# Layer out by seven block products of 288 columns in place of eight, and a new order for the first two batches

## The chip, the cores and the metric

The kernel runs on one core of one Trainium2 chip. The time is device microseconds of one launch. The engines are TensorE (PE; its weight loads are PEld), VectorE (DVE), ScalarE (ACT), GpSimd (POOL) and SyncE (SP), which issues the DMAs. Each engine works through its own instructions in order.

## What is computed

An attention over 32 packed queries, an attention of the long queries over the packed result, and an expert layer with a maximum of three products:

```python
p_packed = sm_attn(p, k, v)                  # 8 batches, 8 heads, 576 keys, 32 packed, 64 wide
out = sm_attn(q, p_packed, p_packed)         # 576 queries per head
x = out.transpose(0, 2, 1, 3).reshape(8 * 576, 512)
h = np.maximum(np.maximum(x @ w1, x @ w2), x @ w3)   # 768 hidden
return h @ w_out                                      # 768 -> 512
```

`sm_attn` is softmax attention with scale 1/8. All is float32. The last line, `h @ w_out`, is what the text calls Layer out; the three products before it are Layer in.

## The kernel before

The eight batches go through the same stages one after another, with the stages of the next batch laid between the matmuls of this one. Results are kept transposed: columns are the 576 tokens of a batch, rows the features.

- **Attention.** `scores` (S) multiplies packed queries and keys, `weigh` (A) takes the softmax, `spread` (X) or `turn` transposes it, `values` (V) and `packed` (K) give the packed result, `queries` (Q) multiplies it with the long queries, and `attend` (B) takes their softmax e and turns it, then splits it into a high part (a2h, a copy in the type float32r) and a low part (a2l, the difference). A product of two float32 operands is made of three float32r matmuls: high by high, low by high, high by low.
- **Weights.** `load_w` brings 24 pieces of 512 words by DMA, `convert` (C) turns each into float32 (two ACT instructions, one DVE, one POOL). The pieces of w_out are also split there into `wo_hi` and `wo_lo`.
- **Layer in.** `project` (P) folds the packed result of a batch into the input weights of one hidden slice j (128 of the 768 rows, so j = 0..5); result pw, split into ph and pl. `layer_in` (N) then computes, for each half of 288 columns and each of the three weights, six matmuls of 288 columns into one PSUM bank (tile mi). `maximum` (E) copies the first of three banks out and takes the maximum with the other two (tile hf).
- **Layer out.** `halves` (H) splits the first 512 of the 576 columns of a slice into high and low part; the last 64 columns go into `tails`, where the 64 of all eight batches stand side by side as 512 columns. `layer_out` (O) adds up each of four output blocks of 128 rows over six slices: 4 x 6 x 3 = 72 matmuls of 512 columns a batch (tile mo). They are issued in twelve "thirds" of 6 (`THIRDS`). After the last batch the same 72 matmuls run once more on the tails, as a ninth set. `finish` (F) scales a block out of PSUM and stores it.

PSUM has two double banks (`ps_big`) for attention and projections, and four single banks (`ps_moe`) for mi, mo and some projections.

**Order.** The first two batches are ordered by hand: `START` is a list of words that sets the order on every engine. A word names a stage with its numbers (`N03`: Layer in of batch 0, slice 3) and issues its next step; a trailing v, g or a moves that step's elementwise instruction to DVE, POOL or ACT; `I10` puts ten matmuls of no use ahead of the next step, to keep TensorE running; k, v, q and w words are loads. For batches 2 to 7 only TensorE's order is fixed: `STAGES` gives the tick, counted from the start of a batch, at which each stage of the next batch is due (`S1:7`: scores of the next batch at tick 7; P6 to P8 are slices 0 to 2 of the next batch). A batch has 36 ticks of Layer in, one for each group of six matmuls, and then one for each step of Layer out. `halves` of a slice is begun one tick after its Layer in. The other engines are ordered by the compiler's scheduler, by the order of issue. Each tile comes from a pool with a tag; the tiles of one tag share a fixed number of buffers, and a new tile waits until one is free.

## Time and profile before

| | us |
|---|---|
| median of 3 runs | 482.0 |
| lowest and highest | 481.85, 482.4 |
| span of the profiled execution | 480.7 |
| outside the span (482.0 - 480.7) | 1.3 |
| busy PE, DVE, ACT, POOL | 471.3, 254.1, 192.5, 130.6 |

The span runs from the first to the last instruction of one execution. The profiled execution has no time of its own beside its span, so the median of the runs stands for it. Rows of the profile give a line of the code, the engine, the operation and "out<-in" by tile names; busy times are in us, means in ns. "idle before" tells how long the engine waited and for which engine. A piece of the chain of waits reads: start, length, engine, tile, line, number of instructions.

### The profile page before, as it was taken

What the parts mean: (1) busy time and instruction counts of PE and PEld (TensorE: products, weight loads), DVE (VectorE), ACT (ScalarE), POOL (GpSimd) and SP (SyncE); (2) the same over time, 40 slices, a digit from 0 to 9 for tenths busy, and PEclk for the clock granted to TensorE, in tenths of its full rate; (3) what the DMA queues carried; (4) which work ended last, traced back from release to release, by engine and by line L of the source; (5) the groups of instructions that cost most, each with busy time, mean ns of one, the idle gap of its engine ahead of it and who ended that gap; (6) DMA issues with size and microseconds to landing.
All of it is one profiled execution on the core that took longest, in us unless ns stands there. A gap on an engine that the chain in (4) does not pass through costs nothing.

```text
span 480.7 us, 10562 instructions
## 1 busy us (share of the span) xinstructions
PE 471.3 (98%) x4352; PEld 388.8 (81%) x4352; DVE 254.1 (53%) x546; ACT 192.5 (40%) x415; POOL 130.6 (27%) x108
## 2 busy tenths in 40 slices
PE   8889999999999999999999999999999999999997
PEld 3367999888778887899789887899778887899885
DVE  2899988833646465453726455363826456244100
ACT  3687854401344334432434325342434324343211
POOL 0666754600322222122212213122222214244000
PEclk9999999999999999999999999999999999999999
DMA  8999221664244152233313142243310201100122
GB/s 302 399 376 407 95 87 65 219 176 147 74 164 128 34 176 81 82 98 110 122 66 125 36 145 100 73 120 107 124 68 12 40 2 45 44 1 1 44 67 65
DMA packets 36767, 55.60 MB, mean 116 GB/s; under 512 B 21488, under 2 KB 23792, under 8 KB 36720
## 3 DMA queue, kind: packets, MB, share of 16 engines
q1 hardware_dynamic: 36720, 54.93, 34.3%
q8 instruction: 34, 0.56, 0.5%
q14 instruction: 13, 0.11, 0.1%
HBM read 41.94 MB, written 9.44 MB: 107 GB/s over the span
## 4 chain that ended last, share of the span: by engine, by line
PE 93%; DMA 5%; ACT 0%; SPq 0%; issue 0%; DVE 0%; ACTq 0%
PE mi L450 48%; PE mo L504 32%; PE pw L414 7%; DMA wi<-in_wi 2%; PE av L312 2%; PE s L341 2%; DMA q<-in_qt 1%; DMA v<-in_va 1%; PE s L226 1%; PE tp L312 0%; PE tp L269 0%; SPq L160 0%; ACT wi L189 0%; PE av L327 0%; ACT a L244 0%
## 5 line engine op out<-in xcount | busy, mean ns | idle before, releaser
L450 PE MATMUL mi<-a2h,ph 128*128 128x288 f32 x576 | 174.1, 302 | 0.0
L450 PE MATMUL mi<-a2h,pl 128*128 128x288 f32 x576 | 169.8, 295 | 0.3 <-DVE pl L427 0.3
L450 PE MATMUL mi<-a2l,ph 128*128 128x288 f32 x576 | 169.7, 295 | 0.0
L465 DVE TENSOR_TENSOR hf<-mi,hf 128x288 f32<-128x288 f32 x192 | 86.6, 452 | 108.1 <-PE mi L450 90.3
L504 PE MATMUL mo<-h,wo_hi 128*128 128x512 f32 x432 | 140.3, 398 | 0.0
L450 PEld LDWEIGHTS mi<-a2h,ph 128*128 128x128 f32 x576 | 108.0, 188 | 14.6 <-issue 9.2
L450 PEld LDWEIGHTS mi<-a2h,pl 128*128 128x128 f32 x576 | 108.1, 188 | 1.0 <-DVE pl L427 0.7
L450 PEld LDWEIGHTS mi<-a2l,ph 128*128 128x128 f32 x576 | 108.1, 188 | 0.0
L131 POOL TENSOR_TENSOR h<-hf,h 128x512 fp32r<-128x512 f32 x36 | 46.6, 1295 | 214.8 <-ACT h L126 119.9
L504 PEld LDWEIGHTS mo<-h,wo_hi 128*128 128x128 f32 x432 | 81.0, 187 | 26.1 <-issue 4.2
L504 PE MATMUL mo<-h,wo_lo 128*128 128x512 f32 x216 | 85.3, 395 | 0.0
L427 DVE SCALAR_TENSOR_TENSOR pl<-pw,ph 128x768 fp32r<-128x768 f32 (+1 forms) x60 | 45.9, 788 | 26.8 <-ACT ph L425 26.6
L126 ACT COPY hf<-mi 128x288 f32<-128x288 f32 x83 | 33.0, 398 | 62.7 <-PE mi L450 57.7
L126 ACT CAST h<-hf 128x512 fp32r<-128x512 f32 x45 | 27.8, 620 | 69.4 <-DVE hf L465 69.4
L524 ACT ACTIVATE o<-mo 128x512 f32<-128x512 f32 x32 | 19.1, 597 | 75.7 <-PE mo L504 58.2
L425 ACT ACTIVATE ph<-pw 128x768 fp32r<-128x768 f32 (+1 forms) x60 | 38.3, 680 | 25.4 <-PE pw L414 25.3
L504 PEld LDWEIGHTS mo<-h,wo_lo 128*128 128x128 f32 x216 | 40.5, 188 | 8.9
L414 PE MATMUL pw<-w_sb,pt 64*32 64x384 f32 x768 | 38.1, 488 | 0.7 <-ACT a L244 0.7
L204 POOL TENSOR_TENSOR w_sb<-w_sb,wi 128x512 int32<-128x512 int32 x18 | 24.1, 1348 | 26.7 <-DVE w_sb L200 18.7
L370 POOL TENSOR_TENSOR e<-e,m 128x576 f32<-128x576 f32 (+1 forms) x15 | 16.7, 1129 | 34.2 <-DVE m L368 34.2
L131 POOL TENSOR_TENSOR a2l<-et,a2h 128x576 fp32r<-128x576 f32 (+1 forms) x13 | 17.5, 1346 | 21.0 <-ACT a2h L126 20.9
L414 PEld LDWEIGHTS pw<-w_sb,pt 64*32 64x32 f32 x768 | 12.0, 106 | 13.3 <-issue 10.6
(91 smaller groups left out, 338.6 us busy)
## 6 DMA issues: line engine op xcount, KB each, us to landing
kt<-in_kp SPq DMA_DIRECT2D x16, 640.0 KB, 5.0
wi<-in_wi SPq DMA_DIRECT2D x18, 512.0 KB, 7.8
out_t<-o SPq DMA_DIRECT2D x35, 256.0 KB, 2.0
v<-in_va SPq DMA_DIRECT2D x16, 512.0 KB, 4.6
q<-in_qt SPq DMA_DIRECT2D x14, 576.0 KB, 5.8
wo<-in_wo SPq DMA_DIRECT2D x6, 512.0 KB, 6.9
xt<-x SPq DMA_DIRECT2D x48, 40.0 KB, 2.0
xt<-x SPq DMA_DIRECT2D x48, 32.0 KB, 1.9
```

Of the source, the lines that this page charges most:

```text
L126: e.copy(out=out, in_=src)
L131: on(default).tensor_tensor(out=lo, in0=src, in1=hi.bitcast(F32), op=ALU.subtract)
L204: nc.gpsimd.tensor_tensor(out=dst.bitcast(I32), in0=dst.bitcast(I32), in1=up, op=ALU.add)
L312: nc.tensor.matmul(out=ps[r][NP * i:NP * i + NP, :], lhsT=at[r][0:n, t, i], rhs=loaded["v", b, g][0:n, t, h * D:(h + 1) * D], start=(t == ...
L370: on("g").tensor_tensor(out=e3, in0=e3, in1=m.unsqueeze(2).to_broadcast([P, nt, NP]), op=ALU.subtract)
L414: nc.tensor.matmul(out=ps[r][NP * n:NP * n + NP, 0:NW * P], lhsT=pt_sb[b % 2][o, NP * n:NP * n + NP], rhs=w_sb[o, j, n * NW * P:(n + 1) * ...
L425: nc.scalar.activation(out=hi[:, r], in_=x, func=AF.Copy, scale=2.0 ** -WS)
L427: nc.vector.scalar_tensor_tensor(out=lo[:, r], in0=x, scalar=2.0 ** -WS, in1=hi[:, r].bitcast(F32), op0=ALU.mult, op1=ALU.subtract,)
L450: nc.tensor.matmul(out=sums[b, j, hf, x][:, 0:HS], lhsT=w[:, r, x * P:(x + 1) * P], rhs=a[:, c], start=(r == 0 and n == 0), stop=(r == R - ...
L465: nc.vector.tensor_tensor(out=h, in0=sums[b, j, hf, i][:, 0:HS], in1=h, op=ALU.max)
L504: nc.tensor.matmul(out=sums[b, m], lhsT=w[:, j, m * P:(m + 1) * P], rhs=h[:, a], start=(j == 0 and i == 0), stop=(j == NJ - 1 and i == 2),)
L524: nc.scalar.activation(out=o, in_=ps, func=AF.Copy, scale=2.0 ** -WS)
```

## The change

Layer out multiplies a matrix of 512 x 768 with one of 768 x 576 per batch. Each pair of slices, both output halves (256 rows) and both column halves (288) make a 2 x 2 block product. In place of its 8 block products, 7 products of sums and differences of blocks are computed (a Strassen scheme with 15 additions), each added up over the three slice pairs.

- `weights` (W) makes the seven combinations of each pair's weight blocks once, with their high and low parts.
- `maximum` writes the four blocks of a slice pair into one tile r. `halves` makes, after the even slice, one difference and the high and low part ya (2 blocks); after the odd slice yb (2 blocks), two instructions of differences, and yc (3 blocks).
- `layer_out` issues fourteen steps, seven products by two halves of 128 rows, of 9 matmuls with 288 columns, in the order 1, 5, 2, 6, 7, 4, 3. Products 1 and 5 read ya, 2 and 3 yb, 6, 7 and 4 yc.
- `finish` scales products 1 and 5 out of PSUM on ACT, adds the others to earlier results on DVE, and makes two more sums on POOL.
- All 576 columns of a batch are covered, so `tails` and the ninth set are gone.
- The pool has new tags: `b` (8 buffers) for k, v, q, the turned softmax and r; `y` (21) for attention, ya, yb and the results; `xs` (6) for loaded weights and later for the weight combinations; `yt` (6) for yc.
- `START` and `STAGES` are new. In the new `START` the fourteen steps of batch 0 lie between and behind the last Layer in steps of batch 1, and the fourteen of batch 1 at its end.

The removed bodies of `halves`, `layer_out` and `finish`, printed above, are left out of the diff; so are changes of a tag alone.

```diff
-SM = SF * P
 SR = S - SF * P
+NQ = NJ // 2
+MH = DM // 2
 NT = S // NP
 NW = 3
 WC = 512
-NST = 4
 WS = 8
+NX, NB, NY = 6, 8, 21
...
-k01 k00 w00 I10 S0 A01 v00 v01 w02 C00 A01 A00 A00 I7 A01 A01v A00 q000 q010 C00 w01 I1 V01 C00 C00 A00v
-Z00 Z01 q011 C02 V01 V00 q001 V00 w21 K0 K0v C02 C01 I1 Q0 C02 B000 B000 B010 C01 C02 B010 B000g C01
-B000 B010v w11 w10 B000 w12 I8 Q0 B000a B010 C21 B001 B000 C21 C01 I3 P00 B011 B000g B001 B001g P00 B011
-B000 C21 B011v B000a B000g C21 B001 B011 B010 B001 B010a B011 B010 k10 k11 C10 B001a w20 P00 I10 N00
-B011a B001 B011 B001v B010v w32 w22 C10 C11 C10 I4 S1 B011v B010 B001 C12 C11 B010a C10 B011 B010v C11
-C12 P00 C12 P00 B001a C20 N00 A10 N00 B011a v11 v10 C20 C11 A11 C12 A10 w40 A11 P01 B001v q10 q11 E000v
-B011g E000 Z11 P01 C32 C32 C20 Z10 C20 A10 N00 N00 P01 C32 A10v A11 N00 C22 A11a E001v C40 C22 E000 V101
-E001 V101 C32 N01 w30 w31 K1 C22 w61 E001 C22 C40 K1a H00a N01 w62 Q1 C30 E010v C40 H00v B11 B10 C40 C30
-H00v N01 C30 C30 C31 N01 E010 B10 P02 P02 E010 C31 P10 B10g E011v w42 P02 N01 w63 C31 N01 B11 C61 w41
-C31 E011 w60 B10 C42 E011 N02 C42 N02 P03 H01a N02 C42 N02 B10 E020v C42 B10v E020 H01g P03 C41 E021a
-N02 N02 B11g E020 P03 C41 E021 H01v C41 N03 N03 C41 P10 B10 P10 E021 H02v E030v C61 B11 B11 E030 N03 w52
-w51 w50 P11 P04 B10g C61 B11v C52 C62 E030 N03 C62 P04 C50 H02g N03 P04 B11 C63 H02a E031a B10 E031 N03
-B10a N04 N04 E040a B11g C51 N04 E031 B11 E040 B10v C51 C51 B11a N04 B11v C50 C52 E041a N04 N04 H03a C61
-E040 E041 E041 N10 H03v C62 C50 C52 H03a E100v H04a P11 N10 N10 C50 E100 C51 P11 E100 N10 C63 E101a N10
-N10 N11 E101 H04v H04a E110v N11 N11 E110 C52 P05 P12 E101 N11 N11 P05 C61a H10a P05 E111a C60 P12 C62
-E110 N11 C61g H10v E111 N05 E111 H11v P12 C60 C62a H10a E050a N05 N05 E050 N05 N12 E051v H11g E050 C62v
-N05 N05 P13 P14 E051 N12 H11v E051 C60 E120a P14 H05v C63 N12 w64 w65 P13 H05g E120 C63 C60 N12 N12 N12
-P13 E121a C65 E120 H05v N13 C63v E121 E121 E130a H12a q21 k20 k21 C64 C60a C65 P14 C64 N13 N13 C63g H12g
-C60g E130 N13 P15 E131a E130 C64 P15 N13 N13 H12a C65 P15 E131 C64 N14 N14 S2 C64v E131 N14 N14 C65
-E140v A20 O0 A21 C65v E140 E140 C65g C64v A20 A21 v21 q20 k30 X2 v20 X2 N14 O0 O0 O0 k31 E141v N14 O0 X2
-O0 F00v E141 E141 Z21 O0 O0 O0 F01a O0 O0 F02a O0 N15 H13a F03v H13v H13a N15 N15 V201 E150v Z20 V201
-N15 K2 N15 E150 N15 K2v E151v E150 E151 Q2 O1 O1 O1 B21 E151 H15a O1 B20 B21 H14a B20 H14v H15g O1 v31
-O1 O1 B20v B21g B21 B20 O1 B20 P20 F10a B21 B21a v30 O1 O1 F11a B20a B20 B20g q31 B20 O1 H15v B21 q30
-B21g B20a P20 B21 P20 B20g B21a O1 B21v F13a H14a F12v
+k00 k01 I10 S0 A01 w02 w00 v00 C02 C02 A01 q010 A00 v01 A00 I7 A01 q000 A00 A01v A00v C02 q001 V01 C00 C00 V00
+Z01 V01 Z00 V00 K0 K0v I1 Q0 w01 B000 C02 B010 C00 C01 C01 C01 q011 B010 B010 B010 B000 B000v B000 k10 C01 I8
+Q0 B011 k11 B001 B001 B000 B000v w12 B010 C12 B000 B000 w11 I4 S1 v10 C00 I3 P00 B000 B000g v11 B001 w10 A10
+A10 B001 B011 B011 B011 B010v q10 q11 A11 B010 P00 B001 B001 P00 P00 w21 A11 P00 k20 B010g B010 C12 C12 B000
+I10 N00 C12 k21 A10 w20 Z10 B011 A10 w22 B010v B010 B011v B011 A11 A11 V101 B011g B001 C10 B001 w30 N00 C11
+Z11 V101 C10 C10 C10 B011 C11 C11 C11 B001 B001v K1 B001 K1 Q1 B10 B011 B11 E000v C21 w32 B011v N00 E000 P01
+P01 B11 C21 N00 N00 N00 P01 C21 S2 C21 E000 E001v E001 C20 C20 C20 C20 A20 C22 C22 N01 w42 N01 C22 E010 A20
+w31 A21 E001 A21 C30 E010 C22 N01 N01 E010 w40 B10 C30 w41 P02 P02 C30 E011v P10 N01 P02 E011 C32 C32 N01 N02
+C30 N02 C32 C32 C31 C31 C31 E011 X2 P10 C40 C40 N02 N02 w51 C31 B11v P10 E020v B10 C41 C41 C41 w50 P03 w62 C42
+C42 C42 E020 v21 P03 C40 P11 P03 C50 E021 N02 N02 C41 v20 w52 E021 N03 E020 C40 N03 C51 E021 C42 B10 P04 E030v
+C51 C51 w64 B10 w63 B11 B11 B11v X2 H00 C51 E030 N03 B10 B10 B11 P04 P04 H00g N03 E031 E030 N03 N03 E031 H01g
+B11g X2 E031 N04 C64 B10 B10 B10g B10 H00 C52 N04 N04 B11 E040 N04 E040 E040 C50 B11v B11v C50 N04 P11 P11 C50
+C63 C52 E041 C64 N04 N10 N10 E100 E100 w60 E041 C62 C63 C62 E041 H04 C52 H02 N10 N10 C52 w65 Z20 Z21 E101 N10
+H02 C63 N10 N11 V201 C60 q20 P05 P05 C63 C62 E101 N11 V201 K2 K2 E101 C64 C64 E110v E110 P05 E100 q21 C62 H04v
+W1v W1 H02v W1 N11 N11 E111 C65 C65 C65 N11 N11 E110 w61 Q2 B21 H03g C65 W1 W1 N05 N05 C60 B20 E050 N05 E050
+H03v W2v W2v C61 C61 P12 C61 P12 P13 E111 C60 P13 N05 E051 N05 N05 P12 E051 E051 N12 C61 B20 C60 E111 N12 E050
+P14 E120v N12 E120 P13 E120 W1 W1 H01v W0 W2 W2 H04 W0 B20v H01 P14 W0v W0g W0 H03v P14 N12 N12 N12 W1 N13 W2v
+W2 W0v P20 H01 P15 E130 E121v E121 E121 N13 N13 E130 W0 N13 E131 E130 W1g W2v W2v H03 P15 P15 N13 k30 N13 E131
+E131 N14 B20 N14 N14 E140 O0 H03g N14 H05v F0 E140 B20 B20v N14 N14 E141 N15 E141 E141 E140 O0 F0 O0 B21 B21
+O0 B21 H13g H05 H05 H03v H05 N15 H01v E150 H01v B21 E150 N15 N15 E150 E151 W1v W0 H14 B20 H05g W2 H10v H10v
+B21v B21 F0 N15 E151 P20 N15 E151 H14g H15 O0 O0 H05v O0 H13v W0g H11 F0 F0 O0 F0 W0v H12 O0 W2 F0 H11 F0 B21
+O0 O0 F0 F0 O0 F0 F0 F0 F0 O0 O0 H12 H14 H10v H11v H11 H12v B20 H13 O1 H15v H15v H15v H13 H13v F1 O1 O1 H13
+H15v F0 H11 F0 H11v H15v F1 F1 O1 O1 F1 B21 O1 F1 F1 O1 F1 O1 O1 F1 F1 k31 B21 B21v P20 B20 B20v O1 O1 B20v O1
+O1 F1 F1 F1 F1 F1 O1 F1 F1
 """
-EXTRA = "12 05 13"
-STAGES = "S1:7 P3:7 k2:10 X1:12 P4:18 P5:18 V1:29 K1:33 v2:32 Q1:37 P6:37 q2:39 P7:43 P8:43"
+STAGES = "S1:7 P3:7 v1:9 X1:12 P4:18 P5:18 q1:26 V1:29 k2:31 K1:33 Q1:36 P6:40 P7:40 P8:45"
...
-        if j < 2:
-            t = pool.tile([P, WC], I64, name=f"wi{j}_{c}", tag="h", bufs=NJ + 1)
-        elif j < NJ:
-            t = pool.tile([P, WC], I64, name=f"wi{j}_{c}", tag="stage", bufs=NST)
-        else:
-            t = pool.tile([P, WC], I64, name=f"wo{c}", tag="kv", bufs=4)
+        t = pool.tile([P, WC], I64, name=f"wi{j}_{c}", tag="xs", bufs=NX)
         nc.sync.dma_start(out=t, in_=wi[j, c] if j < NJ else wo[c])
...
-            dst = pool.tile([P, S], F32, name=f"wof{c}", tag="o", bufs=2)[:, 0:DM]
+            if c // 2 not in blocks:
+                blocks[c // 2] = pool.tile([P, 4, MH], F32, name=f"xb{c // 2}", tag="b", bufs=NB)
+            k = 2 * (c % 2)
+            dst = blocks[c // 2][:, k:k + 2].rearrange("p a m -> p (a m)")
...
-        if j == NJ:
-            yield 2
-            copy(wo_hi[:, c], dst)
-            yield 1
-            split_lo(wo_lo[:, c], dst, wo_hi[:, c])
+    blocks, x_op = {}, {}
+    def weights(p):
+        x = blocks[p]
+        t = pool.tile([P, 2, MH], F32, name=f"xt{p}", tag="y", bufs=NY)
+        hi, lo = [pool.tile([P, 7, MH], F32R, name=f"x{n}{p}", tag="xs", bufs=NX) for n in "hl"]
+        x_op[p] = hi, lo
+        def combine(out, a, b, op):
+            on("g").tensor_tensor(out=out, in0=a, in1=b, op=op)
+        def split(c, src):
+            copy(hi[:, c], src)
+            yield 0
+            split_lo(lo[:, c], src, hi[:, c])
+            yield 0
+        combine(t[:, 0], x[:, 1], x[:, 3], ALU.add)
+        yield 0
+        combine(t[:, 1], t[:, 0], x[:, 0], ALU.subtract)
+        yield 0
+        combine(x[:, 1], x[:, 0], x[:, 1], ALU.subtract)
+        yield 0
+        yield from split(slice(0, 4), x)
+        yield from split(slice(4, 6), t)
+        combine(t[:, 0], x[:, 2], t[:, 1], ALU.subtract)
+        yield 0
+        yield from split(slice(6, 7), t[:, 0:1])
...
-        if j == 0 and b not in (1, 2) or j == 3 and b >= 2:
+        if j == 0 and b == 0 or j == 3 and b >= 2:
...
-        if (b, j) not in hidden:
-            hidden[b, j] = pool.tile([P, S], F32, name=f"hf{b}_{j}", tag="h_f", bufs=2)
-        h = hidden[b, j][:, c]
+        if (b, j // 2) not in hidden:
+            hidden[b, j // 2] = pool.tile([P, 4, HS], F32, name=f"r{b}_{j // 2}", tag="b", bufs=NB)
+        h = hidden[b, j // 2][:, 2 * (j % 2) + hf]
...
+    def operands(b, p, name, c):
+        h = hidden[b, p][:, c]
+        n = c.stop - c.start
+        tag, bufs = ("y", NY) if n == 2 else ("yt", 2 * NQ)
+        hi = pool.tile([P, n, HS], F32R, name=f"{name}h{b}_{p}", tag=tag, bufs=bufs)
+        copy(hi, h)
+        yield 1
+        lo = pool.tile([P, n, HS], F32R, name=f"{name}l{b}_{p}", tag=tag, bufs=bufs)
+        split_lo(lo, h, hi)
+        hid[b, p, name] = hi, lo
+        yield 1
     def halves(b, j):
...
+        r = hidden[b, j // 2]
+        less = lambda out, x, y: on("g").tensor_tensor(out=out, in0=x, in1=y, op=ALU.subtract)
+        if j % 2 == 0:
+            less(r[:, 1], r[:, 1], r[:, 0])
+            yield 1
+            yield from operands(b, j // 2, "ya", slice(0, 2))
         else:
...
+            yield from operands(b, j // 2, "yb", slice(2, 4))
+            less(r[:, 1], r[:, 3], r[:, 1])
+            yield 1
+            less(r[:, 0::2], r[:, 1:2].to_broadcast([P, 2, HS]), r[:, 0::2])
+            yield 1
+            yield from operands(b, j // 2, "yc", slice(0, 3))
+    PRODUCTS = {
+        1: (0, "ya", 0), 2: (2, "yb", 0), 3: (6, "yb", 1), 4: (3, "yc", 2),
+        5: (4, "ya", 1), 6: (5, "yc", 1), 7: (1, "yc", 0),
+    }
+    ORDER = [(n, m) for n in (1, 5, 2, 6, 7, 4, 3) for m in range(2)]
+    def layer_out(b):
+        for n, m in ORDER:
+            x, y, z = PRODUCTS[n]
+            ps = sums[b, n, m] = ps_moe.tile([P, 512], F32, name=f"mo{b}_{n}_{m}", tag="moe")
+            for p in range(NQ):
+                w_hi, w_lo = x_op[p]
+                h_hi, h_lo = hid[b, p, y]
+                for i, (w, h) in enumerate(((w_hi, h_hi), (w_lo, h_hi), (w_hi, h_lo))):
                     nc.tensor.matmul(
...
+                        out=ps[:, 0:HS], lhsT=w[:, x, m * P:(m + 1) * P], rhs=h[:, z],
+                        start=(p == 0 and i == 0), stop=(p == NQ - 1 and i == 2),
                     )
             yield 0
...
+    def finish(b):
+        tiles = {}
+        def temp(name):
+            if name not in tiles:
+                tiles[name] = pool.tile([P, 2, HS], F32, name=f"{name}_{b}", tag="y", bufs=NY)
+            return tiles[name]
+        def scaled(out, n, m):
+            nc.scalar.activation(out=out, in_=sums[b, n, m][:, 0:HS], func=AF.Copy, scale=2.0 ** -WS)
+        def add(out, n, m, x, scale=2.0 ** -WS):
+            nc.vector.scalar_tensor_tensor(
+                out=out, in0=sums[b, n, m][:, 0:HS], scalar=scale, in1=x, op0=ALU.mult, op1=ALU.add,
             )
...
+        def store(x, m, hf):
+            c = slice(hf * HS, (hf + 1) * HS)
+            if b == B - 1 and (m, hf) == (0, 1):
+                for i in range(2):
+                    nc.sync.dma_start(out=out[b, i, :, c], in_=x[:, i])
+            else:
+                nc.sync.dma_start(out=out[b, m:m + 2, :, c].rearrange("m p s -> p m s"), in_=x)
+        for n, m in ORDER:
+            if n == 1:
+                scaled(temp("s")[:, m], n, m)
+            elif n == 5:
+                scaled(temp("t")[:, m], n, m)
+            elif n == 2:
+                add(temp("r")[:, m], n, m, temp("s")[:, m])
+                if m == 1:
+                    store(temp("r"), 0, 0)
+            elif n == 6:
+                add(temp("u")[:, m], n, m, temp("s")[:, m])
+            elif n == 7:
+                add(temp("v")[:, m], n, m, temp("u")[:, m])
+                if m == 1:
+                    yield 0
+                    nc.gpsimd.tensor_tensor(out=temp("u"), in0=temp("u"), in1=temp("t"), op=ALU.add)
+                    yield 0
+                    nc.gpsimd.tensor_tensor(out=temp("t"), in0=temp("v"), in1=temp("t"), op=ALU.add)
+                    store(temp("t"), 2, 1)
+            elif n == 4:
+                add(temp("s")[:, m], n, m, temp("v")[:, m], -2.0 ** -WS)
+                if m == 1:
+                    store(temp("s"), 2, 0)
+            else:
+                add(temp("u")[:, m], n, m, temp("u")[:, m])
+                if m == 1:
+                    store(temp("u"), 0, 1)
+            yield 0
...
+            products, ends = layer_out(b), finish(b)
+            for x in ORDER:
                 tick()
...
+                next(products)
+                for _ in range(3 if x == (7, 1) else 1):
+                    next(ends)
```

95 lines of the change are left out of this document (16 added, 79 removed).

## The prediction

> **What bounds the kernel now.** I read first the page's busy times and its chain of waits, then that chain in order of time.
>
> ```profile
> span 480.7 us, 10562 instructions
> PE 471.3 (98%) x4352; PEld 388.8 (81%) x4352; DVE 254.1 (53%) x546; ACT 192.5 (40%) x415; POOL 130.6 (27%) x108
> PE 93%; DMA 5%; ACT 0%; SPq 0%; issue 0%; DVE 0%; ACTq 0%
> ```
>
> TensorE is busy for 98% of the span and 93% of the chain is its work. The DMA part of the chain lies in the first 28 us. So a change pays what it takes off TensorE's queue, less what it adds in waits there. The chain by pieces shows what Layer out (mo) costs beside Layer in (mi):
>
> ```profile
> 174.06 1.40 PE mo L504 x6
> 175.47 1.13 PE s L341 x32
> ...
> 177.24 8.59 PE mo L504 x36
> 185.83 1.45 PE pw L414 x32
> 187.28 7.18 PE mo L504 x30
> ...
> 428.96 14.51 PE mi L450 x108
> 443.47 33.61 PE mo L504 x144
> ```
>
> Batch 2's Layer out is 6 + 36 + 30 = 72 matmuls of 512 columns in 17.17 us. The last group is 144 of them in 33.61 us, 0.2334 us each: 72 for batch 7 and 72 for the tails, the last 64 columns of all eight batches gathered into one more set of 512. The 108 mi matmuls have 288 columns and cost 14.51 / 108 = 0.1344 us each. Those are the two prices of the sum. A third view, busy time by stretch, shows how loaded the helpers are:
>
> ```profile
> 0.00:24.00 24.00, 19.63 (x200) 9.08 (x201) 12.81 (x40) 12.02 (x27) 8.77 (x14) 1.00 0.95 351
> 24.00:60.00 36.00, 34.55 (x420) 27.44 (x420) 34.06 (x81) 29.61 (x57) 24.48 (x20) 1.00 0.77 293
> 60.00:140.00 80.00, 80.00 (x684) 66.29 (x683) 50.16 (x99) 27.63 (x57) 26.69 (x20) 1.00 0.41 133
> ...
> 194.46:248.89 54.43, 54.43 (x532) 45.98 (x531) 27.99 (x59) 20.69 (x47) 11.59 (x9) 1.00 0.32 99
> ```
>
> The columns after the length are PE, PEld, DVE, ACT, POOL, then clock, DMA share, GB/s. The clock is 1.00 throughout. In a later batch (54.43 us) DVE is half idle and POOL nearly four fifths idle. From 24 to 60 us DVE has 34.06 of 36 us full: in the first two batches it is nearly as tight as TensorE.
>
> **TensorE's part of the change.** Removed are 9 x 72 = 648 matmuls of 512 columns. From the pieces: batch 0 16.80 us (1.40 + 4.20 + 11.20) and batch 1 17.17 (11.39 + 5.78), whose rows follow, batches 2 to 6 17.17 each, and 33.61; together 153.4 us.
>
> ```profile
> 94.43 1.40 PE mo L504 x6
> ...
> 96.63 4.20 PE mo L504 x18
> ...
> 101.63 11.20 PE mo L504 x48
> ...
> 120.42 11.39 PE mo L504 x48
> ...
> 132.61 5.78 PE mo L504 x24
> ...
> 139.83 5.75 PE mi L450 x42
> ```
>
> Added are, for each batch, 7 products x 2 output halves x 3 slice pairs x 3 split matmuls = 126 of 288 columns: 1008 x 0.1344 = 135.5 us. The difference is **-17.9 us**. Per batch there is almost none: 126 x 0.1344 = 16.9 against 16.8 to 17.2. An eighth fewer products is eaten by covering 576 columns in place of 512; the gain is the tail group of 16.8 us that falls away at the end. For bounds I take the slowest and fastest mi pieces of any length:
>
> ```profile
> 194.46 5.55 PE mi L450 x42
> ...
> 201.79 9.05 PE mi L450 x66
> ```
>
> 5.55 / 42 = 0.1321 gives -20.2, 9.05 / 66 = 0.1371 gives -15.2. Both contain stage changes; the unbroken 108 are the nearest row.
>
> Against smaller matmuls speaks a rule of the Trainium skill ("TensorE: Matmul & The Clock Gate", "The mechanism"): a weight load overlaps running matmuls only when it aims at another row group. The trace disagrees: the next rows are 108 matmuls beside 108 full-height loads of 188 ns in 14.51 us, where the loads alone, end to end, would be 20.3.
>
> ```profile
> 428.96:443.47 14.51, 14.51 (x108) 14.28 (x108) 1.00 0.00 1
> ...
> L450 PEld LDWEIGHTS mi<-a2h,pl 128*128 128x128 f32 x576 | 108.1, 188 | 1.0 <-DVE pl L427 0.7
> ```
>
> **Helpers in batches 2 to 7.** Prices are from these rows, by column where the width differs:
>
> ```profile
> L465 DVE TENSOR_TENSOR hf<-mi,hf 128x288 f32<-128x288 f32 x192 | 86.6, 452 | 108.1 <-PE mi L450 90.3
> ...
> L131 POOL TENSOR_TENSOR h<-hf,h 128x512 fp32r<-128x512 f32 x36 | 46.6, 1295 | 214.8 <-ACT h L126 119.9
> L126 ACT CAST h<-hf 128x512 fp32r<-128x512 f32 x45 | 27.8, 620 | 69.4 <-DVE hf L465 69.4
> ...
> L131 POOL TENSOR_TENSOR a2l<-et,a2h 128x576 fp32r<-128x576 f32 x11 | 15.7, 1427 | 20.4 <-ACT a2h L126 20.4
> L370 POOL TENSOR_TENSOR e<-e,m 128x576 f32<-128x576 f32 x13 | 15.4, 1199 | 34.1 <-DVE m L368 34.1
> ...
> L131 DVE TENSOR_TENSOR h<-hf,h x12: 676/692/1822, 38.9 to 444.7; 128x512 fp32r<-128x512 f32 x12
> ```
>
> POOL costs 1295 / 512 = 2.53 ns a column, DVE 692 / 512 = 1.35. Each slice pair now needs differences and low parts of 288 + 576 and 576 + 288 + 576 + 864 = 3168 columns, 8.0 us on POOL; three pairs 24.0, two final sums 2.9, the next batch's attention 5.3 (two a2l, two e - m). That is 32 of 54 us. DVE gains ten additions of about 0.45 us, 32 of 54. Both fit, and the products' evictions (0.45 us for each 1.2 us of matmuls) fit the four PSUM banks.
>
> What can be late is the last pair. From Layer in's end (t = 0): maximum to 0.5; POOL's difference to 1.2 while ACT copies yb (0.7); yb's low part to 2.7; the wide difference to 4.1; ACT's copy of 864 columns to 5.1; the last low part to 7.3. Products 1 and 5 need none of it. Product 2 starts at 4.8 in batch 7; product 6, the first that wants yc, at 7.3, its third pair at 8.1. So batch 7 has about 1 us to spare, of which I give back 0.4 for hand-offs. In the other batches queries (1.13) and two projections (1.45) lie before product 6, some 2.6 us more; the next batch's two e - m subtractions on POOL (1.2 each) take most of that. Cost taken: 0; bounds 0 to 1 us a batch. The next batch's a2l then ends some 3 us later, which its slack holds: in this profile it ended at 242.2, and the Layer in that reads it began at 248.9.
>
> ```profile
> 239.35 2.87 POOL L131 TENSOR_TENSOR a2l<-et,a2h 128x576 fp32r<-128x576 f32 x2 [4.07 <-ACT a2h L126]
> ...
> 248.89 5.55 PE mi L450 x42
> ...
> q<-in_qt SPq DMA_DIRECT2D x14, 576.0 KB, 5.8
> ```
>
> The loads move nearer to their use: v from most of a batch ahead to 20 ticks, q to 10, where a tick is 0.8 us of Layer in or more. Both q loads go out by SP in order, ahead of the k loads at tick 31, and land 5.8 us after issue: 8 us or more of cover, 2 to spare. The eight shared buffers serve 11 tiles a batch; the q tiles wait for the first pair's, which is free once its yc is done, some 8 us after tick 12. If a buffer comes later than that, queries start late, behind them the next attention; cost taken 0, and that too is within the 1 us a batch above. After the last matmul come one addition and one store, as now: 0.
>
> **The first two batches.** Here lies the risk. TensorE's useful work there stays (28 products of 1.2 us for 24 thirds of 1.4, all else the same), but the helpers' does not. Counting the letters behind each word of the order, two-input work on operands and weights goes on POOL from 5,120 columns to 16,352 (+28.4 us), on DVE from 4,096 to 13,408 (+12.6 us); DVE gets 20 additions (+9.0) and loses about 1 elsewhere. POOL also gets 6,656 columns of copies. No row shows a POOL copy; between DVE's cast (0.83 ns a column, from 426 ns for 512) and POOL's subtraction these are 5.5 to 16.8 us; I take 10.6, by POOL's own 205 ns memset of 128 columns:
>
> ```profile
> masks.py:197 POOL MEMSET ident<- 128x128 f32 x1 | 0.2, 205 | 0.3 <-POOLq L674 0.3
> ...
> L128 DVE CAST h<-hf x3: 420/426/426, 52.1 to 79.3; 128x512 fp32r<-128x512 f32 x3
> ```
>
> Nearly all of it falls into 60 to 140 us. There DVE goes from 50 to 71 of 80 us, POOL from 27 to 66. And the two don't run side by side:
>
> ```profile
> 66.53 1.82 DVE L131 TENSOR_TENSOR h<-hf,h 128x512 fp32r<-128x512 f32 x1
> ...
> 63.89 3.91 POOL L204 TENSOR_TENSOR w_sb<-w_sb,wi 128x512 int32<-128x512 int32 x3 [4.70 <-ACT ph L425]
> 67.76 1.76 POOL L204 TENSOR_TENSOR wof<-wof,wo 128x512 int32<-128x512 int32 x1
> ```
>
> DVE's subtraction of two SBUF tensors, 0.69 us alone, took 1.82: POOL's third conversion ran until 67.8, and the next one then took 1.76 in place of 3.91 / 3 = 1.30. They took turns. The Trainium skill says so ("SBUF — State Buffer", "Who interferes with whom"): DVE's second SBUF input and POOL's reads share one port, held for a whole instruction. The trace agrees. Then POOL's 66 us and DVE's 18 us of such work (13,408 x 1.35) queue for one place: 84 of 80 us. Some 3 us (batch 1's last sums) may end later and some start before 60, so the demand is just at the limit. I take **+3.5 us** as bubbles of two in-order queues at that load. Below: -3, because the new order puts batch 1's scores ahead of the first projection, where TensorE idles (24.00 - 19.63 = 4.4 us in the first stretch). Above: +13, by the dear POOL copies (+6) and waits of 7 more.
>
> **Sum.** 480.7 span + 1.3 outside it = the median of 482.0. 482.0 - 17.9 + 3.5 + 0.4 = **468.0 us**.
>
> **The rivals.**
> - The start hides all its new work or gains: 461 to 465 us. For it: POOL may run ahead of TensorE in the first 60 us, and TensorE has no gap from 60 to 140 us now. Chance 0.22.
> - The forecast, 465 to 473: 0.49.
> - The start is bound by POOL and DVE taking turns, +8.5 to +16: 473 to 480.5. For it: the 84 of 80. Chance 0.18.
> - The products don't do what they say: no cheaper per batch than before, and each new bank costs a hand-off, so 3.38 / 24 = 0.1408 us a matmul as in the piece below: 141.9 us, -11.5; about 474. Chance 0.05.
>
> ```profile
> 222.61 3.38 PE mi L450 x24
> ```
>
> - Slower: one mechanism in Layer out of batches 2 to 7, at product 6. If POOL takes the next batch's attention ahead of the last low part, yc comes at about 12 to 15 us and not 8 to 10. Each batch then waits up to 4 us; the sign turns when six waits eat the 14 us of gain, 2.3 us each: 483 to 492. Against it: by the sum above POOL is some 60% busy there and keeps 1 to 3 us of slack. Chance 0.05.
> - Weight loads that can't overlap, by the skill's rule above: 360 more loads x 0.188 = +67.7, 41,472 fewer columns x 0.456 ns = -18.9; about 531 us. The quoted overlap speaks against it. Chance 0.01.
>
> **How the numbers follow.** The likeliest case gives 468.0. The range 461.5 to 476.5 takes the forecast, the hidden start, the dear matmuls and half of the bound start, so about 0.83. A measurement here tells 0.2% (1 us) from no change. Slower: the last two cases, 0.06, of which a little stays inside 1 us: 0.05. Same: 0.01. Faster: 0.94.
>
> **What the profile after would show.** Right: no second group of 72 behind batch 7; mo matmuls as long a spacing as mi, 126 of them in about 17 us; the period from batch to batch still 54.4 us. The start's price is read from where batch 2's Layer in begins (139.8 us now): 143 forecast, 137 to 140 if hidden, over 147 if bound. TensorE waits there should name POOL or DVE low parts and weights. Wrong: TensorE waiting for POOL in every batch at product 6, or spacing above 0.14 us.

## The result: slower by 2.8%, and the profile after

| | before | after |
|---|---|---|
| median (lowest to highest) | 481.96 us (481.85 to 482.4) | 495.42 us (494.57 to 496.3) |
| ratio, 95% interval | | 1.0279 (1.0264 to 1.0293) |
| the profiled execution: span | 480.7 us | 493.3 us |
| batch 2's Layer in begins | 139.83 us | 166.54 us |
| last batch's Layer in begins | 412.16 us | 441.35 us |
| from there to the end of the span | 68.5 us | 51.9 us |

The page of the changed kernel, the same three lines as before:

```profile
span 493.3 us, 11594 instructions
PE 469.0 (95%) x4710; PEld 407.4 (83%) x4710; DVE 319.3 (65%) x625; ACT 192.2 (39%) x374; POOL 286.1 (58%) x229
PE 76%; DVE 12%; DMA 5%; POOL 2%; ACT 2%; issue 2%; SPq 1%; DVEq 0%; ACTq 0%; POOLq 0%
```

Before, 93% of the chain was TensorE. Now it is 76%, and VectorE holds 12%. Where in the span that is, the chain in order of time tells (start, length, what):

```profile
166.54 5.56 PE mi L467 x42
...
221.49 5.57 PE mi L467 x42
...
441.35 5.56 PE mi L467 x42
...
458.32 14.51 PE mi L467 x108
472.83 1.21 PE mo L536 x9
...
479.06 2.06 POOL ycl L125
481.17 8.77 PE mo L536 x64
```

Three differences make up the whole 12.6 us between the spans. The start is longer by 166.54 - 139.83 = **26.7 us**. Batches 2 to 6 take 441.35 - 166.54 = 274.8 us against 272.3: **+2.5**. The end, from the last Layer in on, is shorter by **16.6**: the tail group is gone. 26.7 + 2.5 - 16.6 = 12.6. So the part that the change was worth arrived, and the start cost 1.6 times as much. The stretches of the changed kernel that answer to those shown of before (PE, PEld, DVE, ACT, POOL, clock, DMA share, GB/s):

```profile
60.00:140.00 80.00, 71.27 (x661) 61.85 (x654) 68.44 (x116) 29.84 (x55) 60.51 (x51) 0.98 0.24 75
```

```profile
221.49:276.45 54.96, 54.96 (x585) 49.37 (x585) 32.80 (x68) 21.84 (x43) 31.55 (x25) 1.00 0.33 100
```

In a late batch VectorE and GpSimd have over 20 us to spare and TensorE is full. From 60 to 140 us VectorE is at 68.44 of 80 (before 50.16), GpSimd at 60.51 (before 26.69), and TensorE, full before, stands idle for 8.7 us. The pieces of the chain in the start show what its work hung on:

```profile
58.08 6.82 DMA wi<-in_wo
...
78.23 7.08 DMA q<-in_qt
...
104.64 2.50 DVE xh L122
...
140.46 1.98 DVE yal L125
...
149.14 1.04 DVE ych L122 x2
150.60 13.75 PE mo L536 x90
```

Two kinds are to be seen: from 58 to 85 us the longest pieces that aren't TensorE's are loads (6.82 and 7.08 us), from 87 to 150 us the chain runs again and again through VectorE's sums, copies and low parts. One of those, with GpSimd's work beside it:

```profile
102.33 1.20 POOL L122 CAST xh<-xb 128x1024 fp32r<-128x1024 f32 x1 [0.34 <-DVE xb L208]
102.56 0.94 DVE L444 SCALAR_TENSOR_TENSOR pl<-pw,ph 128x768 fp32r<-128x768 f32 x1
103.43 1.21 DVE L125 TENSOR_TENSOR xl<-xb,xh 128x1024 fp32r<-128x1024 f32 x1
103.62 3.25 POOL L125 TENSOR_TENSOR xl<-xb,xh 128x1024 fp32r<-128x1024 f32 x1
104.56 2.58 DVE L122 CAST xh<-xt 128x512 fp32r<-128x512 f32 x1
```

VectorE's cast of 512 columns took 2.58 us; the kernel before has the same form at 0.42. It ended at 107.14, 0.27 us behind GpSimd's subtraction of 1024 columns, as if it had waited its turn (run b2 below tests that). The eviction behind it on VectorE (a copy out of PSUM) was 2.04 us late for TensorE.

Summed up over the start, TensorE idles 20.8 us of 166.5 (before 5.8 of 139.8): 15.0 of the 26.7. Its five longest waits there stand in the brackets of these rows:

```profile
37.13 0.88 PE L431 MATMUL pw<-w_sb,pt 64*32 64x384 f32 x16 [1.99 <-DVE e L381]
...
69.25 0.40 PE L467 MATMUL mi<-a2h,ph 128*128 128x288 f32 x1 [1.40 <-ACT r L120]
...
85.35 1.58 PE L358 MATMUL s<-q,pt 64*32 64x288 f32 x24 [2.16 <-DMA q<-in_qt]
...
107.56 0.40 PE L467 MATMUL mi<-a2h,ph 128*128 128x288 f32 x1 [2.04 <-DVE r L122]
...
150.60 0.42 PE L536 MATMUL mo<-yah,xh 128*128 128x288 f32 x1 [3.77 <-DVE u L555]
```

From 95 to 151 us TensorE waits eight times, each time for VectorE, 10.1 us in all; the longest is the 3.77 us at 150. Two waits hang on loads, 3.6 us together: 2.16 us at 85 for queries, and 1.40 at 69 for a copy on ScalarE, which had itself stood 2.55 us waiting for an output weight to convert. A wait of 1.99 us at 37 is for VectorE's transpose of the long queries' scores. Some 5 us more are clock. After three of the waits the granted clock fell; this is the first, TensorE alone by microsecond (busy, clock, DMA share, GB/s):

```profile
35.00:36.00 1.00, 0.14 (x2) 1.00 1.05 407
36.00:37.00 1.00, 0.00 (x0) 1.00 1.03 406
37.00:38.00 1.00, 0.87 (x17) 1.00 1.00 393
38.00:39.00 1.00, 1.00 (x7) 0.60 1.00 401
39.00:40.00 1.00, 1.00 (x6) 0.50 1.07 426
40.00:41.00 1.00, 1.00 (x6) 0.50 0.45 180
41.00:42.00 1.00, 1.00 (x6) 0.69 0.17 70
42.00:43.00 1.00, 1.00 (x33) 1.00 0.33 74
```

A wait of 1.99 us, and then half the clock for some 3.4 us: 0.40 + 0.50 + 0.50 + 0.31 = 1.7 us lost on top. The same 1.7 us follow the waits of 2.16 us at 85 and 3.77 us at 150. The Trainium skill ("TensorE: Matmul & The Clock Gate", "HAM oscillation — how this bites in real kernels") names idle gaps of over about 3.4 us as what drops the clock; here gaps of 2 us did it too, though the one of 2.04 us at 107 did not. The remaining 6.6 of the 26.7 us lie in time that the profile counts as busy; they weren't taken apart.

### The profile page after: what moved, and what is told of

The parts are those of the page before. It is cut to its first block, busy times and chain, and to the rows that moved or that the text cites. A ratio compares the mean times of both kernels' runs of the same rounds, so it can differ in the third digit from the quotient of the medians.

```text
span 493.3 us, 11594 instructions
## 1 busy us (share of the span) xinstructions
PE 469.0 (95%) x4710; PEld 407.4 (83%) x4710; DVE 319.3 (65%) x625; ACT 192.2 (39%) x374; POOL 286.1 (58%) x229
## 4 chain that ended last, share of the span: by engine, by line
PE 76%; DVE 12%; DMA 5%; POOL 2%; ACT 2%; issue 2%; SPq 1%; DVEq 0%; ACTq 0%; POOLq 0%
PE mi L467 41%; PE mo L536 23%; PE pw L431 6%; DMA v<-in_va 2%; PE av L329 2%; PE s L358 2%; DMA q<-in_qt 1%; PE s L243 1%; DMA wi<-in_wo 1%; DVE r L481 1%; DVE r L505 1%; DVE ybl L125 1%; DVE ycl L125 1%; DVE pl L444 1%; ACT wi L178 1%
## 5 line engine op out<-in xcount | busy, mean ns | idle before, releaser
L481 DVE TENSOR_TENSOR r<-mi,r 128x288 f32<-128x288 f32 x192 | 86.3, 453 | 79.5 <-PE mi L467 72.6
L505 POOL TENSOR_TENSOR r<-r 128x288 f32<-128x288 f32 (+1 forms) x67 | 71.3, 1065 | 78.1 <-DVE r L481 75.7
L120 ACT COPY r<-mi 128x288 f32<-128x288 f32 x88 | 35.1, 399 | 117.5 <-PE mi L467 117.4
L125 POOL TENSOR_TENSOR ycl<-r,ych 128x864 fp32r<-128x864 f32 x19 | 39.2, 2065 | 8.5 <-ACT ych L120 6.1
L536 PE MATMUL mo<-ych,xh 128*128 128x288 f32 x144 | 43.6, 303 | 0.0
L536 PE MATMUL mo<-ych,xl 128*128 128x288 f32 x144 | 42.6, 296 | 0.0
L536 PE MATMUL mo<-ycl,xh 128*128 128x288 f32 x144 | 42.4, 295 | 0.1
L125 POOL TENSOR_TENSOR ybl<-r,ybh 128x576 fp32r<-128x576 f32 x20 | 29.5, 1476 | 11.8 <-ACT ybh L120 11.6
L125 POOL TENSOR_TENSOR yal<-r,yah 128x576 fp32r<-128x576 f32 x21 | 30.2, 1439 | 8.6 <-ACT yah L120 8.6
L536 PE MATMUL mo<-yah,xh 128*128 128x288 f32 x96 | 29.2, 304 | 3.8 <-DVE u L555 3.8
```

The costliest lines, as they stand in the source:

```text
L120: e.copy(out=out, in_=src)
L125: on(default).tensor_tensor(out=lo, in0=src, in1=hi.bitcast(F32), op=ALU.subtract)
L481: nc.vector.tensor_tensor(out=h, in0=sums[b, j, hf, i][:, 0:HS], in1=h, op=ALU.max)
L505: less = lambda out, x, y: on("g").tensor_tensor(out=out, in0=x, in1=y, op=ALU.subtract)
L536: nc.tensor.matmul(out=ps[:, 0:HS], lhsT=w[:, x, m * P:(m + 1) * P], rhs=h[:, z], start=(p == 0 and i == 0), stop=(p == NQ - 1 and i == 2),)
```

## The experiments

All times stand beside runs of the kernel before on the same chip, 481.6 to 482.8 us. Those with a ratio come from four to six runs, the others from one; the changed kernel's own four runs lie 1.7 us apart, so a difference of 2 to 3 us in a single run says little. "Start" is the time at which batch 2's Layer in begins: 139.83 before, 166.54 after.

### Is it the helpers' work, and on which engine?

The first three move the new work of the first two batches between engines. In `a1` the rounded copies of weights and operands go to ScalarE; `a2` and `a3` do that too and put all differences, sums and low parts on GpSimd or on VectorE.

```diff
-        less = lambda out, x, y: on("g").tensor_tensor(
+        less = lambda out, x, y: (engine[E or chosen[0] or "g"] if b < 2 else nc.gpsimd).tensor_tensor(
...
+        chosen[0] = "a"
         copy(hi[:, c], src)
```

(`E` is none in a1, "g" in a2, "v" in a3.)

> The changed kernel with the copies of the operands of batches 0 and 1 and of the weights (high parts) all on ACT; 11,232 columns leave DVE and POOL. Everything else keeps its engine and place. In the changed kernel batch 2's Layer in begins at 166.5 us (139.8 before the change). Theory LOAD (DVE and POOL have too much to do in the first two batches, and take turns at their shared way into SBUF): DVE loses about 8 us and POOL about 9, ACT has room (68 of 166 us busy), so batch 2 begins 8 to 14 us earlier and the time falls from 495 to about 481 to 487. Theory ORDER (each queue is in order, and it is the place of single instructions that makes TensorE late, whatever the load): less than 4 us either way.

> As a1, and all differences and low parts of these operands and weights go to POOL (29,760 columns less the final sums there, none on DVE). If DVE's own work is the bound, DVE falls from about 136 to 105 us busy before batch 2, and batch 2 begins before 150 us. If the shared way is the bound (POOL is slower per column, 2.53 against 1.35 ns), the sum of turns grows by about 13 us less the copies, and batch 2 begins no earlier than in a1, and at 165 to 175 us. Theory ORDER: within 6 us of a1.

> As a1, and all differences and low parts of these operands and weights go to DVE, none to POOL. DVE has then about 22 us more work than in a1, POOL about 38 less, and there are far fewer turns. If DVE's own work is the bound: batch 2 begins at 170 us or later. If the turns with POOL are the bound: at 150 us or earlier. Theory ORDER: within 6 us of a1.

Measured: a1 492.05 us, start 163.64 (-2.9); a2 502.01, start 173.63 (+7.1); a3 497.32, start 168.99 (+2.5). With all on GpSimd, TensorE's two longest waits are for GpSimd's low parts (3.78 and 3.05 us; the first stretch below is a2's). With all on VectorE the longest is for VectorE (4.61 us for a projection's low part; the second stretch, a3's):

```profile
100.00:160.00 60.00, 46.95 (x305) 42.88 (x305) 19.96 (x38) 20.12 (x38) 50.55 (x42) 0.86 0.09 31
```

```profile
100.00:140.00 40.00, 33.08 (x256) 29.53 (x255) 31.37 (x62) 18.41 (x33) 1.16 (x1) 0.91 0.08 25
```

In a3 GpSimd is idle, so nothing takes turns, and TensorE still loses 7 of 40 us. The turns are thus not the whole cause; no division of this work that was tried fits into the start.

Next, work was left out. `a4` makes no low parts of the operands in batches 0 and 1 and reads the rounded part twice, `b2` makes none of the weights, `b1` makes neither, nor the differences. TensorE's matmuls stay the same.

```diff
-        lo = pool.tile([P, n, HS], F32R, name=f"{name}l{b}_{p}", tag=tag, bufs=bufs)
-        split_lo(lo, h, hi)
-        hid[b, p, name] = hi, lo
+        if b < 2:
+            hid[b, p, name] = hi, hi
...
-        x_op[p] = hi, lo
+        x_op[p] = hi, hi
```

(The first edit is that of a4, the second, in the weights, that of b2; b1 has the like of both, `less` does nothing in its first two batches, and its operands' rounded copies go to ScalarE. b1 and b2 also need three tiles fewer from the six buffers of tag xs.)

> The changed kernel without the low parts ya, yb, yc of batches 0 and 1 (the high part is read in their place, so the matmuls stay the same). It leaves out 18 instructions on DVE and POOL, by the trace of the changed kernel about 14 us of DVE and 11 us of POOL. Theory LOAD: batch 2 begins 12 to 20 us earlier, at 147 to 155, time 476 to 483. Theory ORDER: less than 6 us earlier. Later batches keep their period of 55.0 us in either.

> The changed kernel without the low parts of the weight combinations alone (9 instructions, by the changed kernel's trace 9 us of POOL and 4 of DVE); the high part is read in their place. Theory LOAD: batch 2 begins 3 to 7 us earlier, near 161. If only the operands' low parts, which come later, are late: less than 2 us.

> The changed kernel, where batches 0 and 1 have neither differences nor low parts of their operands (the copies are on ACT, the high part is read twice) and the weight combinations have no low parts (their high parts are read twice); the matmuls stay the same. It leaves out nearly all the helper work that the change adds to the first two batches. a4, which left out only the operands' low parts, began batch 2 at 153.8 us. If the added work is the whole loss, batch 2 begins at 138 to 142 us. If the new order of the first two batches (attention, conversions, loads) loses by itself what a4's stretch before 100 us still showed (some 13 us), it begins at 148 to 153.

Measured: a4 482.07, start 153.75 (-12.8); b2 492.36, start 164.03 (-2.5); b1 480.06, start 151.70 (-14.8). So 13 to 15 of the 26.7 us go with the work. The rest doesn't: b1 has only the weights' sums and the rounded copies left of it, and is still 11.9 us late. Its chain:

```profile
47.09 4.18 DMA wi<-in_wi
...
58.93 7.92 DMA wi<-in_wo
...
71.19 8.25 PE mi L466 x48
...
151.70 5.57 PE mi L466 x42
```

From 71.19 on TensorE works without a break, and before that the chain passes through 12.1 us of loads of weights. That this is close to 11.9 proves little, since TensorE had other work during most of these loads. Over the whole start of b1 it idles 9.7 us, 3.9 more than before; 2.8 us are waits for copies on ScalarE that stood behind the conversion of staged weights. The clock takes 5.1 us, in three drops of 1.7, one of them right behind these waits. The remaining 2.9 are time counted as busy. So b1 puts some 4.5 us on staged weights, and leaves the rest of its 11.9 without a tested cause.

b2 answers the question of the turn. There GpSimd's subtraction of the weights' low part is left out, and the same cast on VectorE reads:

```profile
104.93 0.41 DVE L122 CAST xh<-xt 128x512 fp32r<-128x512 f32 x1
```

It took 0.41 us in place of 2.58, and TensorE's wait of 2.04 us behind it is gone. So a turn did make that wait, though all of b2 is only 2.5 us earlier.

### Is it the loads?

`d1` puts the two loads for which TensorE waits at 85 us (batch 2's queries) ahead of two weight loads on SP's queue; only words of the order move.

```diff
-... w63 ... w60 ... w65 ... q20 ... q21 ...
+... w63 ... q20 q21 w60 ... w65 ...
```

> The changed kernel with one edit: the two loads of batch 2's queries stand ahead of two of the output weights' loads on SP's queue and no longer behind them. In the changed kernel TensorE waited 2.16 us for them at 85.35 and ran at a clock of 0.72 in the 6 us around it. LATE LOADS (this wait adds to the sum): batch 2's Layer in begins 2 to 4 us earlier than 166.54, the kernel takes 491.5 to 493.5. HELPERS (VectorE and GpSimd, behind which TensorE waits at 95 to 151 us anyway, set when START ends): the wait at 85 goes and comes back later; batch 2 begins at 165.5 to 166.5, 494.5 to 495.5.

A miss for both theories: 498.91 us, start 170.34, 3.8 later. The wait at 85 did go, but the weight loads behind the queries now came late: ScalarE waited 8.67 us for one to convert it, and TensorE 4.12 us, until 86.48, for an eviction behind that. Here one load came earlier at the cost of another.

`c1` asks the question from the other side: the first two batches in the order of before and without the scheme (plain blocks of 288 columns), the scheme from batch 2 on, with the weights' sums made in batch 2, but with the shared buffers of the changed kernel.

```diff
-        "O": layer_out, "F": finish, "W": weights,
+        "O": plain_out, "F": plain_finish,
...
+            if b == 2:
+                for p in range(NQ):
+                    begin(weights(p), clock[0] + WAT[p])
```

> The seven products for batches 2 to 7 alone. Batches 0 and 1 compute Layer out by eight plain block products (144 matmuls of 288 columns each, 19.4 us against 16.9), with the order of the first two batches of the kernel before (its words for Layer out's results moved forward, four loads for batch 3 left to later); the weight combinations are made in batch 2, on DVE, ACT and POOL, from the plain high and low parts. There are no tails. If the first two batches' helper work and order are the whole loss, batch 2 begins at 143 to 148 us (139.8 + 2 x 2.4, and up to 3 for fewer buffers), batch 2 is up to 3 us longer, and the time is 473 to 479 us: faster than both. If the buffers shared by k, v, q and the weights are what delays the start, batch 2 begins at 155 or later and the time is over 485.

494.83 us, start 159.12, of which 4.7 are the blocks' own: 144 matmuls of 288 columns a batch cost 19.4 us (0.1344 each) where 72 of 512 cost 17. TensorE had just two long waits in the start, 6.54 us at 57 and 3.76 at 96. The first, in SP's queue and on ScalarE:

```profile
47.57 11.67 SPq L142 DMA_DIRECT2D wi<-in_wi  x3
62.23 1.21 ACT L177 ACTIVATE wi<-wi 128x512 f32<-128x512 f32 x2 [7.48 <-DMA wi<-in_wi]
```

SP needs 11.67 us to issue three loads: they wait for a free one of six staging buffers, into which four output weights had been loaded ahead of them. ScalarE waits 7.48 us for what they bring, with evictions behind it. Before, input and output weights were staged in different buffers, and the same three loads went out from 42.95 on. `c2` parts them again: the output weights are staged in the eight buffers of tag b.

```diff
-            t = pool.tile([P, WC], I64, name=f"wi{j}_{c}", tag="xs", bufs=NX)
+            tag, bufs = ("xs", NX) if j < NJ else ("b", NB)
+            t = pool.tile([P, WC], I64, name=f"wi{j}_{c}", tag=tag, bufs=bufs)
```

> Like c1_plain_start (the first two batches by 288-column blocks without the scheme, in the order of before; the scheme from batch 2 on), with one edit: the output weights are staged in the 8 buffers of tag b, where the loads of k, v and q go, and no longer in the 6 buffers of xs, which are left to the input weights and, later, to the weights' operands. BUFFERS (the two waits of TensorE in c1's start, 6.54 and 3.76 us, come of input weights whose loads stood behind staged output weights): both waits go, batch 2's Layer in begins at 147 to 151 in place of 159.12, the kernel takes 483 to 487 us. ORDER (the loads had time to spare and something else holds ScalarE): batch 2's Layer in stays at 157 or later, over 492 us. A wait that comes back at the loads of batch 1's k, v and q (ten tiles for eight buffers) would show as a TensorE wait before batch 1's attention instead.

480.31 us, start 144.60: 14.5 us gone by two lines, more than the 10.3 us of the two waits: the granted clock, 0.83 from 60 to 80 us and 0.87 from 100 to 120 in c1, is 1.00 in both stretches of c2. 144.60 is before's 139.83 and the blocks' 4.7: nothing else is lost. Here the loads are shown as a cause. For the changed kernel itself, whose order differs, the edit wasn't tried; its trace shows the two waits of 3.6 us together, with one drop of the clock behind the second, some 5 us.

### Where do the weights' sums belong?

In c2 batch 2 still took 62.3 us, 7.3 more than a later one, for the sums that stand in it. `c3` begins them later in batch 2, and `c6` is c3 once more.

```diff
-WAT = 1, 11, 21
+WAT = 6, 16, 26
```

> c2_wo_staging with the sums of the weights (made in batch 2 here) begun 6, 16 and 26 steps into batch 2 in place of 1, 11 and 21. In c1 they stood ahead of TensorE's helpers on VectorE and cost waits of 1.36, 0.60 and 2.57 us (a sum of 256 columns took 2.28 us there, in turns with GpSimd). TURNS: spread out they cost less: 1 to 3.5 us under c2. If the waits only move, the same as c2 within 1 us.

> c3_wo_staging_late_sums once more, timed in five rounds: 476.3 +/- 0.5 as in its single run, a ratio to the kernel before of 0.987 to 0.990. If the single run was a chance, 478 or more.

c3 476.28 us; c6 476.32 (476.14 to 476.47), ratio 0.9876 (0.9861 to 0.989). Batch 2 takes 58.4 us. `c4` moves the sums back into the start, into batch 0's Layer out, where GpSimd did nothing, and puts them on GpSimd; only the one block that the plain products still read is replaced in batch 2.

```diff
-            copy(hi[:, c], src)
+        combine(x, hi[:, 0:4].bitcast(F32), lo[:, 0:4].bitcast(F32), ALU.add)
...
+W0 W0 W0 W0 W0 W1 W1 ...
```

> c3_wo_staging_late_sums with the sums of the weights moved back, out of batch 2 into the Layer out of batch 0 (97 to 122 us), where GpSimd was idle for 20 of 20 us and VectorE for 15: the sums and low parts on GpSimd alone, the rounded copies on ScalarE. Only the one block that the plain products still read is replaced in batch 2. In c3 batch 2 took 58.36 us from its first Layer in to batch 3's (144.48 to 202.84), 3.4 more than the 54.97 of the batches after it. FREE (work put where its engine idles costs nothing): batch 2 takes 55 to 55.6 us and the kernel 472.5 to 474 us, START as in c3 (144.5 +/- 0.5). COLLIDE (27 us of GpSimd's work make VectorE's maxima and evictions take turns): START grows by 1 to 4 us and the kernel stays at 475 to 477.

494.01 us (ratio 1.0248, 1.0234 to 1.0262), start 165.43, far outside both expectations. The chain tells why:

```profile
113.91 0.72 SPq L319
...
124.20 1.95 DMA xt<-x
126.54 2.34 POOL xb L215
...
133.30 0.40 ACT xh L119
133.71 0.32 ACT o L577
134.07 3.25 PE mi L477 x12
```

The third block xb needed a buffer of tag b that the transfers xt<-x still read. These were waiting in turn for the second block's buffer, which GpSimd read until 113.9, and then went out by SP one after the other. GpSimd stood until 126.5, ScalarE's copy of the sum behind GpSimd, an eviction of Layer out behind that copy, and TensorE 13.77 us behind the eviction. Batch 2 itself took no time for sums any more: its Layer out began 35.3 us after its Layer in, 38.6 in c3. `c5` therefore needs no buffer and no other engine: the sums take their terms from the rounded and low parts directly, all on GpSimd.

```diff
+        combine(t[:, 0], h[1], (h[3], add), (l[1], add), (l[3], add))
...
-        copy(hi[:, 4:6], t)
+        nc.gpsimd.tensor_copy(out=hi[:, 4:6], in_=t)
```

> c4_sums_in_start without the two things that its trace shows as its wait of 13.77 us: the sums take their terms straight from the rounded and the low parts (no block xb, and so no buffer of tag b, which came free there only after the transfers of xt), and the rounded copies go on GpSimd too, so that no eviction on ScalarE stands behind a sum. Some 31 us of GpSimd's work from 96 us on, 3 x (10 sums of 256 columns at 0.74 and 2.7 for copies and low parts). QUEUES (the sums themselves cost nothing there, only what stood behind them): batch 2's Layer in begins at 144.5 to 146, batch 2 takes 55 to 55.6, the kernel 472.5 to 475. COLLIDE (GpSimd and VectorE in turns): START grows by over 2 us and the kernel stays over 476.

478.16 us (475.93 to 479.77), ratio 0.991 (0.9886 to 0.9935): batch 2 in 55.2 us, but the start at 149.44, with a wait of 2.93 us for a low part of batch 1 that stood behind the sums:

```profile
131.70 1.36 POOL hl L124
133.11 7.50 PE mo L569 x43
```

`c7` issues the sums one instruction at a time and spreads the third block's over the steps of batch 1's Layer out.

```diff
-... O0 W2 W2 O0 W2 ...
+... O1 W2 ... O1 W2 ... O1 W2 ...
```

> c5_sums_on_pool_alone with the third block's sums one by one behind the twelve steps of batch 1's Layer out, and not in one piece ahead of it. In c5 GpSimd did the sums from 96.75 to 131.7 without a pause, a low part of batch 1 (hl) that stood behind them ended at 133.1, and TensorE waited 2.94 us for it. QUEUES: that wait goes, batch 2's Layer in begins at 144.5 to 146.5 in place of 149.4, batch 2 stays at 55.1, the kernel takes 472.5 to 475. COLLIDE (the attention of batch 2 takes turns with the sums instead): the loss moves into batch 1's Layer out or batch 2's first projection and the kernel stays at 476 to 479.

**473.04 us** (472.9 to 473.53), ratio to before **0.9817** (0.9804 to 0.9831). The wait is gone. Page and chain of c7:

```profile
span 471.4 us, 11628 instructions
PE 460.9 (98%) x4748; PEld 406.7 (86%) x4748; DVE 282.8 (60%) x591; ACT 193.8 (41%) x380; POOL 280.9 (60%) x241
```

```profile
144.61 5.75 PE mi L481 x42
...
199.77 5.57 PE mi L481 x42
...
419.64 5.57 PE mi L481 x42
```

Against before: start +4.8, batches 2 to 6 in 275.0 us (+2.7), the end -16.8; together -9.3, as the spans say (480.7 to 471.4). GpSimd is busy for 92.1 us of the start here, not much less than in the changed kernel (100.4), and in c7's stretch from 96 to 122 us for 21.78 of 26 with TensorE full:

```profile
96.00:122.00 26.00, 26.00 (x278) 25.40 (x285) 8.94 (x23) 2.93 (x7) 21.78 (x30) 1.00 0.33 95
```

So GpSimd's amount of work alone needn't cost TensorE anything; in c4 and c5 it was what stood behind it in the queues. For VectorE c7 shows no such thing: it is busy for 98.9 us of c7's start, about as before the change (97.0), against 135.9 in the changed kernel.

## Why the prediction was wrong

**Right.** The tail group went as forecast: -16.6 at the end, where 16.8 us of matmuls fell away. The last pair's chain held within 1 us: the last low part ended 8.3 us after Layer in's end (481.12 against 472.83; forecast 7.3, and 0.4 for hand-offs), and TensorE lost 0.3 us on it, at the third pair of product 6, where the prediction had it. Batches 2 to 7 stay TensorE's, with VectorE and GpSimd idle for some two fifths. The demand on the helpers in the start was well counted: VectorE 71 forecast, 68.44 measured, GpSimd 66 and 60.51. The case that the start is "bound by POOL and DVE taking turns" was named among the rivals, and the sign to look for was the right one: batch 2 "over 147 if bound". Its price, +8.5 to +16, fits the 13 to 15 us that go with the work, but only in part for its reason: b2 shows one such turn, and a3, with hardly any, is no faster.

**Mis-sized, small.** The products were put at 16.9 us a batch. They take 4.96 + 4.96 + 1.47 + 6.18 = 17.57 us in batch 6 of the changed kernel, 0.139 us each and not 0.1344: stage changes cut them into four pieces, where the price came from an unbroken run. Against the 17.17 us of before that is 0.4 of the +0.5 a batch. Weight loads did hide behind the matmuls: in the changed kernel too, 108 matmuls with a load each take 14.51 us. The prediction quoted a rule of the Trainium skill on them ("TensorE: Matmul & The Clock Gate", "The mechanism"). Another sentence of that section lets a load into the background weight buffer go ahead of running matmuls as well; the traces show the overlap, not the buffer.

**Wrong.** The step that failed is the price of the first two batches: "I take +3.5 us as bubbles of two in-order queues at that load", bounds -3 to +13. It measured +26.7. Three things were missing from it.

- The load was right and its price was not. A demand of 84 for 80 us was turned into 3.5 us of bubbles. In the changed kernel 13 to 15 us go with this work (a4 -12.8, b1 -14.8); the trace shows them as TensorE's waits for VectorE from 95 to 151 us, 10.1 us and one drop of the clock. No division among the engines that was tried was cheap (a1 -2.9, a2 +7.1, a3 +2.5).
- The loads of the start were not priced at all. The prediction weighed the shared buffers for batches 2 to 7 alone ("The eight shared buffers serve 11 tiles a batch"). In the start the weights went from several sets of buffers to six that input weights, output weights and their sums share, and SP issues in order. In before's order that cost 14.5 us (c1 to c2). In the changed kernel the trace shows some 5 us of it: waits of 3.6 us and one drop of the clock.
- The clock. It was 1.00 throughout before, and the prediction gave it no term. Three drops behind waits cost 5.1 us, two of them counted above already.

The upper bound of +13 held dearer copies on GpSimd (+6) and 7 us of waits; the start cost twice that.

What stays open: the share of the work in the changed kernel comes from leaving it out, that of the loads is read from waits, and neither was cured there. By the trace some 10 of the 26.7 us are left without a tested cause; 3.7 of them are the wait for VectorE at 37 and the drop of the clock behind it. Whether the scheme could also run in batches 0 and 1 without loss, with weights staged apart and the sums spread as in c7, wasn't tried; it would save about the 4.8 us by which c7's start is late.

## What to carry to other kernels

Where a stage has every engine near its limit, new work there isn't paid by its bubbles at the average load: count first what each queue would hold up (loads behind buffers, evictions behind copies), and put the work into a stage where the engine's row shows idle time and nothing urgent stands behind it, in pieces small enough to stand between what TensorE waits for. When buffers are merged, follow every load of the start through the merged pool, in the order in which they are issued: two lines of staging were worth 14.5 us in c2. And keep a change where it pays: the scheme's gain lay in the tail group, and was to be had without the first two batches.

## Not expected of the hardware

- A cast on VectorE, with one float32 input from SBUF, waited its turn behind GpSimd as two-input work does: 2.58 us for 512 columns beside GpSimd's subtraction, 0.41 without it (b2). The prediction counted only two-input work ("DVE's 18 us of such work").
- GpSimd's cast took 0.61 us for 512 columns in c5, 1.2 ns a column; the prediction took 10.6 us for 6,656 columns, 1.6 ns each.
- The granted clock halved for about 3.4 us after waits of 1.99, 2.16 and 3.77 us, but not after each of this length: 2.04 us in the changed kernel and 1.99 us in b1 left it at 1.00.
- GpSimd at 21.78 of 26 us cost TensorE nothing where VectorE was busy for 9 us, mostly with copies and maxima out of PSUM: c3 and c7 pass 96 to 122 us with TensorE full, with 0 and 21.78 us on GpSimd.
